# Retention and an ELU feed-forward layer: where the load and the attention of unit 3 stand among the weight loads and FFN1

## The chip, the cores and the metric

The kernel runs on one core of one Trainium2 chip. The metric is the device time of one execution in microseconds (us), the median of several runs. The profile is of one execution, and its times count from the start of its span.

## The reference

Two layers follow each other. The first is a retention: causal attention without a softmax, in which the score of a query and a key is weakened by a head's decay to the power of their distance. The second is a feed-forward layer with an ELU between two matrix products.

```python
# q, k, v: (8 batches, 8 heads, 576 positions, 64), float32
scores = 1/sqrt(64) * matmul(q, k.transpose(0, 1, 3, 2))
gamma = 1.0 - 2.0 ** (-5.0 - arange(8))              # one decay per head
rel = pos[:, None] - pos[None, :]
Dmat = where(rel >= 0, gamma[:, None, None] ** rel, 0.0)
ret = matmul(scores * Dmat, v)
x = ret.transpose(0, 2, 1, 3).reshape(4608, 512)     # tokens by heads * 64
h = x @ w_in                                         # w_in (512, 2048)
g = where(h > 0, h, exp(minimum(h, 0)) - 1)          # ELU
out = g @ w_out                                      # w_out (2048, 512), out float32
```

## The kernel before

The 4608 tokens are 36 units of 128 tokens. The attention of a unit has these steps: `load` (q, k and v of all heads, three or six transfers issued on SyncE), `cast` (q and k to bf16), `scale_v` (v times a decay, on GpSimd), `turn` (transposes of q and k on TensorE and the copies back), `scores`, `masks` (the causal mask and the move out of PSUM, on VectorE), `inter` (the part from earlier units through a state), `state` (its update), `intra` (the product of masked scores and v), `put_x` (the result times a decay, into the input of the feed-forward layer) and `state_out` (the state, copied for the next unit). The feed-forward layer takes units in groups; `ffn1` computes tiles of h with the ELU, and `ffn2` the products with w_out. In FFN1 of group 0 (units 0 to 2) each of the 16 tiles is 128 of the 2048 features by 384 tokens, and four tiles use one part of w_in.

```python
GROUPS = [[0, 1, 2], [3], [4], [5], [6, 7], [8, 9], [10, 11, 12], [13, 14, 15]]
GROUPS += [list(range(u, u + 4)) for u in range(16, NU, 4)]
raw = ctx.enter_context(tc.tile_pool(name="raw", bufs=8))
ps_h = ctx.enter_context(tc.tile_pool(name="ps_h", bufs=3, space=PSUM))   # ps_m, ps_s, ps_o, ps_st: 1 each
# ... (cut)
def load(u, after=None):
    qk = raw.tile([P, 2, H, D], FP32, name="rqk", tag="rqk")
    vv = raw.tile([P, H, D], FP32, name="rv", tag="rv")
    if after is not None:
        after.memset(qk[0:1, 0, 0, 0:1], 0.0)          # the load waits for this engine's place in order
    for p0, b, s0, n in place(u):
        for dst, src in ((qk[p0 : p0 + n, 0], q), (qk[p0 : p0 + n, 1], k), (vv[p0 : p0 + n], v)):
            nc.sync.dma_start(dst, src[b, :, s0 : s0 + n, :].rearrange("h p d -> p h d"))
# ... (cut)
def load_w_in(n):                                      # 512 of 2048 columns, float32 to bf16 on the way
    s = slice(n * 512, (n + 1) * 512)
    nc.gpsimd.dma_start(w_in_sb[:, :, s], w_in_v[:, :, s])

def load_w_out(c, f0, f1):                             # 256 of 512 columns
    s = (slice(None), slice(f0, f1), slice(c * 256, c * 256 + 256))
    nc.gpsimd.dma_start(w_out_sb[s], w_out_v[s])

for u in range(4):
    load(u)
# ... (cut)
def stretch(u, ahead=True):                            # attention of a unit, later in the kernel
    ahead = ahead and u + 1 < NU
    if ahead:
        scores(u + 1)
    inter(u); state(u); intra(u)
    if ahead:
        masks(u + 1)
    put_x(u)
    state_out(u)
# ... (cut)
def ffn1(g, ft, bank=None):
    pool, tag = bank or (ps_h, "ph")
    ph = pool.tile([P, 512], FP32, name="ph", tag=tag)
    # ... 4 matmuls for each 128 features
    nc.scalar.activation(e[:, w], ph[:, w], AF.Exp)
    nc.gpsimd.tensor_scalar(m[:, w], e[:, w], -1.0, 1.0, ALU.add, ALU.mult)
    # g = min(max(ph, 0), m) on VectorE, issued up to three slots later
# ... (cut)
def dummy(n):                                          # matmuls without use, 512 columns each
    dum = ps_m.tile([P, 512], FP32, name="dum", tag="pm")
    for _ in range(n):
        nc.tensor.matmul(dum, warm[:, :P], warm, start=True, stop=True)

def product(u):
    inter(u); state(u); intra(u); put_x(u); state_out(u)
# ... (cut)
dummy(18)
cast(0, A, V); make_gx(); scale_v(0); turn(0, h); dummy(2)
for u in range(3):
    scores(u); inter(u); state(u); masks(u)
    if u < 2:
        cast(u + 1, A, G)
        if u == 0:
            load_w_in(0)
        scale_v(u + 1); dummy(3); turn(u + 1, h)
    else:
        for n in range(1, 4):
            load_w_in(n)
        load_w_out(0, 0, 8); load_w_out(0, 8, 16); load_w_out(1, 0, 16)
        dummy(3)
    intra(u); put_x(u); state_out(u); dummy(2)
cast(3, A, V)

for n in range(16):
    f1(0, n, m if n % 4 == 3 else None)                # one tile of FFN1 of group 0
    if n == 3: turn(3)
    if n == 5: scale_v(3)
    if n == 7: scores(3); masks(3, 0)
    if n == 8: masks(3, 1)
    if n == 9:
        load(4, nc.vector)
        for u in range(5, 12):
            load(u)
    if n == 11: product(3)
for n in range(4):
    f1(1, n, m if n == 3 else None)
finish()
for u, bank in enumerate((h, h, h, m)):
    ffn2_half(u, 0, bank)                              # FFN2 of units 0 to 3, columns 0 to 255
prep(4, A, G)                                          # cast and scale_v
ffn2_half(0, 1, h); turn(4); ffn2_half(1, 1, h); scores(4); masks(4); prep(5, A, G)
ffn2_half(2, 1, h); product(4); turn(5); ffn2_half(3, 1, m)
scores(5); masks(5); prep(6, A, G)
f1(2, 0); f1(2, 1); turn(6); f1(2, 2)
# then a list of slots: FFN1 of a group alternates with FFN2 of the group before it,
# and the attention of later units is put between them by a timetable (due, events)
```

(Statements that stand on lines of their own in the kernel are joined here with semicolons.)

Of the kernel before, what the change touches and what calls it, by code (L numbers as in the profile page):

```python
# [9 lines left out]
FP32 = mybir.dt.float32  # L10
# [7 lines left out]
def kernel(  # L18
# [9 lines left out]
    nc = tc.nc  # L28
# [4 lines left out]
    P = 128  # L33
# [66 lines left out]
        nc.gpsimd.dma_start(w_out_sb[s], w_out_v[s])  # L100


    for u in range(4):
        load(u)

    ident = const.tile([P, P], BF16, name="ident")
# [180 lines left out]
            xts[g][:, :, i * P : (i + 1) * P], os_[u], gx[:, :, s0 : s0 + P], ALU.mult  # L287
        )

    def stretch(u, ahead=True):  # L290

        ahead = ahead and u + 1 < NU
        if ahead:
            scores(u + 1)
        inter(u)
        state(u)
        intra(u)
        if ahead:
            masks(u + 1)
        put_x(u)  # L300
        state_out(u)


# [41 lines left out]
    def ffn2(g, s):  # L345
        it, part = divmod(s, 4)
        while late and (g, part * 4 + 3) >= late[0][4]:
            finish(slot[0] - late[0][0])
        if part == 0:
            pool, tag = ((ps_o, "o"), (ps_m, "pm"), (ps_h, "ph"))[it] if g == NG - 1 else (ps_m, "pm")  # L350
# [30 lines left out]

    V, A, G = nc.vector.tensor_copy, nc.scalar.copy, nc.gpsimd.tensor_copy

    def dummy(n):
        dum = ps_m.tile([P, 512], FP32, name="dum", tag="pm")
        for _ in range(n):
            nc.tensor.matmul(dum, warm[:, :P], warm, start=True, stop=True)  # L387

# [28 lines left out]
    for u in range(3):  # L417
        scores(u)
        inter(u)
        state(u)  # L420
        masks(u)
        if u < 2:
            cast(u + 1, A, G)
            if u == 0:
                load_w_in(0)
            scale_v(u + 1)
            dummy(3)
            turn(u + 1, h)
        else:
            for n in range(1, 4):  # L430
                load_w_in(n)
            load_w_out(0, 0, 8)
            load_w_out(0, 8, 16)
            load_w_out(1, 0, 16)
            dummy(3)
        intra(u)
        put_x(u)
        state_out(u)
        dummy(2)
    cast(3, A, V)  # L440


    def f1(g, n, bank=None):
        k = 512 // (P * len(GROUPS[g]))
        ffn1(g, k * n, bank)

    for n in range(16):
        f1(0, n, m if n % 4 == 3 else None)
        if n == 3:
            turn(3)  # L450
        if n == 5:
            scale_v(3)
        if n == 7:
            scores(3)
            masks(3, 0)
        if n == 8:
            masks(3, 1)
        if n == 9:
            load(4, nc.vector)
            for u in range(5, 12):  # L460
                load(u)
        if n == 11:
            product(3)
    for n in range(4):
        f1(1, n, m if n == 3 else None)
    finish()
# [8 lines left out]
    prep(5, A, G)  # L475
    ffn2_half(2, 1, h)
    product(4)
    turn(5)
    ffn2_half(3, 1, m)
    scores(5)  # L480
    masks(5)
    prep(6, A, G)
    f1(2, 0)
    f1(2, 1)
    turn(6)
    f1(2, 2)


    slots, start, now = [(f1, 2, 3, 1.0)], {}, 1.0
    for g in range(3, NG + 1):  # L490
        f1s, f2s = [], [(ffn2, g - 1, s, 1.0) for s in range(4 * len(GROUPS[g - 1]))]
        if g < NG:
            per = 4 // len(GROUPS[g])
            f1s = [(f1, g, s, per * len(GROUPS[g]) / 4) for s in range(NFT // per)]
        else:
            f2s = f2s[:-4]
        a, b = 0, 2 if g == 4 else 0
        slots += f2s[:b]
        now += b
        start[g] = now  # L500
        while a < len(f1s) or b < len(f2s):
            if b * len(f1s) <= a * len(f2s) and b < len(f2s) or a >= len(f1s):
                slots.append(f2s[b])
                b += 1
            else:
                slots.append(f1s[a])
                a += 1
            now += slots[-1][3]
    due = {5: 0.0}
    last = 5  # L510
    for g in range(4, NG):
        u1 = GROUPS[g][-1]
        for u in range(last + 1, u1 + 1):
            due[u] = due[last] + (start[g] - 1.0 - due[last]) * (u - last) / (u1 - last)
        last = u1
    events = []
    for u in range(5, NU):
        def at(share):
            return due[u] + share * (due[u + 1] - due[u])
        events.append((due[u], 0, u))  # L520
        if u + 2 < PE_TURNED:
            events += [(due[u], -1, u + 2), (at(0.5), 1, u + 2)]
        if PE_TURNED <= u + 3 < NU:
            events.append((at(0.4) if u + 2 < PE_TURNED else due[u], -1, u + 3))
    events.sort()

    now = 0.0
    for f, g, s, d in slots:
        while events and events[0][0] <= now + d / 2:
            _, kind, u = events.pop(0)  # L530
            if kind == -1:
                prep(u, *((A, G) if u < PE_TURNED else (V,)))
                if u >= PE_TURNED:
                    turn(u)
            elif kind == 1:
                turn(u)
            else:
                load_next()
                stretch(u)
# [34 lines left out]
```

## Time and profile before

| | before |
|---|---|
| median of 3 runs | 319.48 us (318.46 to 320.52) |
| span of the profiled execution | 318.0 us |
| granted TensorE clock, mean | 0.993 |
| first tile of FFN1 starts | 17.56 us |
| first product of FFN2 starts | 37.92 us |
| TensorE busy from 17.56 to 37.92 us | 17.85 of 20.36 us |

The page names the engines PE (TensorE), PEld (its weight loads), DVE (VectorE), ACT (ScalarE), POOL (GpSimd) and SP (SyncE); SPq and POOLq are the issue of transfers. An instruction is given by line of the kernel, operation and tiles: `ph` is FFN1's result in PSUM, `pm` and `pmh` are FFN2's, `dum` a dummy's, `tr` a transpose, `sc` the scores, `o` the attention's result, `st` the state, `xt` the input of the feed-forward layer, `m`, `e` and `g` steps of the ELU, `rqk` and `rv` what is loaded of q, k and v. A bracket at the end of a line gives the idle time before an instruction and who ended it. The page's slices are a fortieth of the span, 7.95 us each; PEclk is the granted clock of TensorE in tenths.

### The profile page before, as it was taken

To read this page: it belongs to the slowest core of one execution; us is meant where nothing else is said; L and a number is where in the kernel's file an instruction comes from. 1 tells how busy PE (TensorE), PEld (TensorE's weight loads), DVE (VectorE), ACT (ScalarE), POOL (GpSimd) and SP (SyncE) were. 2 spreads that over 40 slices of the span, in tenths; PEclk is the share of its full clock that TensorE was granted. 3 is DMA by queue.
4 is the path that set the end of the run, shared out by engine and by line. 5 is a ranking of instruction groups with operands and counts; after the bars stand their busy time and mean duration, and the time that the engine had idled before them with its cause. 6 is when DMAs were issued, how large, how long until landed. Compare 5 with 4: busy or idle time off the path is not lost.

```text
span 318.0 us, 7546 instructions
## 1 busy us (share of the span) xinstructions
PE 307.1 (97%) x2974; PEld 174.2 (55%) x3011; DVE 187.4 (59%) x297; ACT 136.9 (43%) x254; POOL 144.9 (46%) x223
## 2 busy tenths in 40 slices
PE   8969999999999999999999999999999999999995
PEld 3535888877766555555444444444444444444444
DVE  2755724667768777776677666666666655444300
ACT  6435514654643444444444444344444444344411
POOL 2875633555645655544554444444444433333300
PEclk9998999999999999999999999999999999999999
DMA  9999999999999998999999859778224200000111
GB/s 170 215 220 201 197 206 253 205 202 202 207 233 188 233 224 179 168 235 195 170 212 170 171 123 207 166 166 170 69 66 69 66 35 33 35 33 33 66 69 66
DMA packets 150195, 48.72 MB, mean 153 GB/s; under 512 B 138640, under 2 KB 146192, under 8 KB 150160
## 3 DMA queue, kind: packets, MB, share of 16 engines
q1 hardware_dynamic: 141888, 41.76, 67.5%
q0 software_dynamic: 6256, 4.19, 8.8%
q10 hardware_dynamic: 2016, 2.29, 2.2%
q8 instruction: 23, 0.38, 0.5%
q14 instruction: 12, 0.10, 0.1%
HBM read 36.70 MB, written 9.44 MB: 145 GB/s over the span
## 4 chain that ended last, share of the span: by engine, by line
PE 82%; DMA 6%; issue 3%; POOL 3%; SPq 2%; DVE 2%; ACT 0%; POOLq 0%; DVEq 0%
PE ph L329 35%; PE pm L354 31%; PE pmh L370 6%; PE sc L211 3%; DMA w_in_sb<-in_moe_w_in_dram 3%; PE o L273 2%; SPq L86 2%; PE st L256 2%; PE o L239 2%; DMA rv<-in_v_dram 2%; DMA qkT<-qkn 1%; POOL m L336 1%; POOL vn L177 1%; DVE pt L223 1%; PE tr L195 1%
## 5 line engine op out<-in xcount | busy, mean ns | idle before, releaser
L336 POOL TENSOR_SCALAR m<-e 128x512 bf16<-128x512 f32 (+1 forms) x156 | 93.7, 601 | 142.0 <-ACT e L334 137.1
L329 PE MATMUL ph<-xt,w_in_sb 128*128 128x512 bf16 (+3 forms) x816 | 146.5, 315 | 3.9 <-DMA w_in_sb<-in_moe_w_in_dram 2.3
L313 DVE SCALAR_TENSOR_TENSOR g<-ph,m 128x512 bf16<-128x512 f32 (+1 forms) x156 | 100.2, 647 | 81.3 <-POOL m L336 80.3
L334 ACT ACTIVATE e<-ph 128x512 f32<-128x512 f32 (+1 forms) x156 | 87.9, 564 | 124.6 <-PE ph L329 119.8
L354 PE MATMUL pm<-w_out_sb,g 128*128 128x512 bf16 x478 | 122.8, 379 | 1.5 <-issue 0.8
L329 PEld LDWEIGHTS <-w_in_sb 128*128 128x128 bf16 x832 | 71.8, 98 | 59.5 <-issue 4.0
L354 PEld LDWEIGHTS <-g 128*128 128x128 bf16 x496 | 47.8, 98 | 53.2 <-issue 0.2
L223 DVE TENSOR_TENSOR pt<-sc,mask 128x1024 bf16<-128x1024 f32 (+1 forms) x37 | 44.2, 1194 | 14.6 <-PE sc L211 14.4
L177 POOL TENSOR_TENSOR vn<-rv,gk 128x512 bf16<-128x512 f32 x36 | 37.9, 1052 | 1.8 <-DMA rv<-in_v_dram 1.3
L286 DVE TENSOR_TENSOR xt<-o,gx 128x512 bf16<-128x512 f32 x36 | 24.5, 682 | 3.1 <-PE o L273 2.9
L361 ACT COPY ot<-pm 128x512 f32<-128x512 f32 x31 | 18.1, 585 | 14.5 <-PE pm L354 13.8
L370 PE MATMUL pmh<-w_out_sb,g 128*128 128x256 bf16 (+1 forms) x176 | 18.3, 263 | 0.0
L265 ACT CAST sb<-st 128x256 bf16<-128x256 f32 x32 | 11.9, 373 | 13.1 <-PE st L256 11.3
L211 PEld LDWEIGHTS <-qkT 64*64 64x64 bf16 x576 | 9.2, 106 | 14.0 <-issue 7.8
L370 PEld LDWEIGHTS <-g 128*128 128x128 bf16 x176 | 15.7, 98 | 1.9
L168 DVE CAST qkn<-rqk 128x1024 bf16<-128x1024 f32 x24 | 16.6, 691 | 0.0
L211 PE MATMUL sc<-qkT 64*64 64x128 bf16 x576 | 15.1, 222 | 0.7 <-ACT qkT L197 0.5
L273 PE MATMUL o<-pt,vn 128*64 128x128 bf16 x288 | 14.4, 222 | 0.0
L375 DVE COPY oth<-pmh 128x256 f32<-128x256 f32 (+1 forms) x6 | 2.4, 400 | 18.0 <-PE pmh L370 18.0
L387 PE MATMUL dum<-warm 128*128 128x512 bf16 x32 | 11.2, 473 | 1.4 <-DVE warm L108 1.3
L239 PE MATMUL o<-qkT,sb 64*64 64x128 bf16 (+1 forms) x256 | 12.3, 214 | 0.0
L197 ACT COPY qkT<-tr 128x512 bf16<-128x512 bf16 x12 | 7.0, 585 | 9.6 <-DVE qkT L196 5.9
(40 smaller groups left out, 90.1 us busy)
## 6 DMA issues: line engine op xcount, KB each, us to landing
rqk<-in_q_dram SPq DMA_DIRECT2D x32, 256.0 KB, 4.7
rqk<-in_k_dram SPq DMA_DIRECT2D x32, 256.0 KB, 5.0
rv<-in_v_dram SPq DMA_DIRECT2D x32, 256.0 KB, 5.1
out_dram<-ot SPq DMA_DIRECT2D x27, 256.0 KB, 2.3
w_in_sb<-in_moe_w_in_dram POOLq DMA_DIRECT2D x4, 512.0 KB, 9.2
out_dram<-oth ACTq DMA_DIRECT2D x9, 128.0 KB, 4.0
w_out_sb<-in_moe_w_out_dram POOLq DMA_DIRECT2D x2, 512.0 KB, 14.6
w_out_sb<-in_moe_w_out_dram POOLq DMA_DIRECT2D x1, 1024.0 KB, 22.9
```

The costliest lines, as they stand in the source:

```text
L177: nc.gpsimd.tensor_tensor(n, rv, gk[:, u % R].unsqueeze(2).to_broadcast([P, H, D]), ALU.mult)
L211: nc.tensor.matmul(sc[j * 64 : (j + 1) * 64, i, hp], t[r, 1, hp, j * 64 : (j + 1) * 64], t[r, 0, hp], start=(hp == 0), stop=(hp == HP - 1) ...
L223: nc.vector.tensor_tensor(pts[u][:, s].rearrange("p i h t -> p (i h) t"), scs[u][:, s].rearrange("p i h t -> p (i h) t"), m.unsqueeze(1).t ...
L239: nc.tensor.matmul(o[rows, hp, :n], sbs[u][rows, hp], qkTs[u][rows, 0, hp, :n], start=(hp == 0), stop=False, skip_group_check=True,)
L273: nc.tensor.matmul(o[i * D : (i + 1) * D, hp], vns[u][:, h], pts[u][:, i, hp], start=(u % R == 0 and hp == 0), stop=(hp == HP - 1), skip_g ...
L286: nc.vector.tensor_tensor(xts[g][:, :, i * P : (i + 1) * P], os_[u], gx[:, :, s0 : s0 + P], ALU.mult)
L313: nc.vector.scalar_tensor_tensor(gt_, ph, 0.0, m, ALU.max, ALU.min)
L329: nc.tensor.matmul(ph[:, i * n : (i + 1) * n], w_in_sb[:, j, f : f + P], xts[g][:, j, :n], start=(j == 0), stop=(j == KJ - 1), skip_group_ ...
L334: nc.scalar.activation(e[:, w], ph[:, w], AF.Exp)
L336: nc.gpsimd.tensor_scalar(m[:, w], e[:, w], -1.0, 1.0, ALU.add, ALU.mult)
L354: nc.tensor.matmul(pm, gts[g, ft][:, it * P : (it + 1) * P], w_out_sb[:, ft], start=(ft == 0), stop=(ft == NFT - 1))
L370: nc.tensor.matmul(pm, gts[g, ft][:, it * P : (it + 1) * P], w_out_sb[:, ft, c0:c1], start=(ft == 0), stop=(ft == NFT - 1),)
```

## The change

It reorders the start of the kernel and the units 3 to 7. Unit 3 is no longer loaded first with units 0 to 2; w_in's second part is issued right after the first, then unit 3, then the third and fourth part from within FFN1, so that the parts of w_in come ahead of what is needed later. The attention of unit 3 is no longer spread over FFN1's tiles: it stands in one piece after tile 7, with eight dummies to keep TensorE at work while the copies and the mask product run. The loads of w_out are issued from within FFN1 rather than before it. Units 5 to 7 get other places for scores, mask product and product; in `stretch` the last unit of a group writes its `xt` before the next unit's mask product; group 2 accumulates FFN2 in a bank of `ps_h`. The arithmetic is the same.

```diff
-    for u in range(4):
+    for u in range(3):
         load(u)
 ...
-    def stretch(u, ahead=True):
+    def stretch(u):
+        if u + 1 < NU:
             scores(u + 1)
         inter(u)
         state(u)
         intra(u)
-        if ahead:
+        last = GROUPS[group_of[u][0]][-1] == u
+        if last:
+            put_x(u)
+        if u + 1 < NU:
             masks(u + 1)
-        put_x(u)
+        if not last:
+            put_x(u)
         state_out(u)
 ...
-            pool, tag = (... if g == NG - 1 else (ps_m, "pm")
+            pool, tag = (... if g == NG - 1 else (ps_h, "ph") if g == 2 else (ps_m, "pm")
 ...
-    def dummy(n):
-        dum = ps_m.tile([P, 512], FP32, name="dum", tag="pm")
+    def dummy(n, bank=(ps_m, "pm")):
+        dum = bank[0].tile([P, 512], FP32, name="dum", tag=bank[1])
 ...
     for u in range(3):
         scores(u)
         inter(u)
-        state(u)
+        if u == 2:
+            load(3, nc.vector)
         masks(u)
         if u < 2:
             cast(u + 1, A, G)
             if u == 0:
                 load_w_in(0)
+                load_w_in(1)
             scale_v(u + 1)
             dummy(3)
             turn(u + 1, h)
         else:
-            for n in range(1, 4):
-                load_w_in(n)
-            load_w_out(0, 0, 8)
-            load_w_out(0, 8, 16)
-            load_w_out(1, 0, 16)
             dummy(3)
+        state(u)
         intra(u)
         put_x(u)
         state_out(u)
         dummy(2)
-    cast(3, A, V)
 ...
-    for n in range(16):
+    o = (ps_o, "o")
+    for n in range(8):
         f1(0, n, m if n % 4 == 3 else None)
+        if n == 0:
+            load_w_in(2)
         if n == 3:
-            turn(3)
-        if n == 5:
-            scale_v(3)
-        if n == 7:
-            scores(3)
-            masks(3, 0)
-        if n == 8:
-            masks(3, 1)
-        if n == 9:
+            load_w_in(3)
+            cast(3, A, V)
+    turn(3)
+    scale_v(3)
+    dummy(3, o)
+    scores(3)
+    masks(3)
+    load_w_out(0, 0, 8)
+    load_w_out(0, 8, 16)
+    dummy(5, o)
+    product(3)
+    for n in range(8, 16):
+        f1(0, n, m if n % 4 == 3 else None)
+        if n == 10:
             load(4, nc.vector)
             for u in range(5, 12):
                 load(u)
         if n == 11:
-            product(3)
+            load_w_out(1, 0, 16)
 ...
     product(4)
+    ffn2_half(3, 1, m)
     turn(5)
-    ffn2_half(3, 1, m)
-    scores(5)
-    masks(5)
     prep(6, A, G)
     f1(2, 0)
     f1(2, 1)
+    scores(5)
+    masks(5)
+    f1(2, 2)
+    f1(2, 3, m)
+    product(5)
     turn(6)
-    f1(2, 2)
-    slots, start, now = [(f1, 2, 3, 1.0)], {}, 1.0
+    slots, start, now = [], {}, 0.0
 ...
-        a, b = 0, 2 if g == 4 else 0
+        a, b = 0, 3 if g == 4 else 0
 ...
-    due = {5: 0.0}
-    last = 5
+    due = {6: 6.0}
+    last = 6
 ...
-    events = []
-    for u in range(5, NU):
+    events = [(0.0, -1, 7), (2.0, 2, 6), (4.0, 1, 7)]      # prep 7, scores and masks 6, turn 7
+    for u in range(6, NU):
```

More of the change, by code (lines that the diff above doesn't have):

```diff
@@ L288, in put_x @@
         )
-    def stretch(u, ahead=True):
-        ahead = ahead and u + 1 < NU
-        if ahead:
+    def stretch(u):
+        if u + 1 < NU:
             scores(u + 1)
@@ L297, in stretch @@
         intra(u)
-        if ahead:
+        last = GROUPS[group_of[u][0]][-1] == u
+        if last:
+            put_x(u)
+        if u + 1 < NU:
             masks(u + 1)
-        put_x(u)
+        if not last:
+            put_x(u)
         state_out(u)
@@ L349, in ffn2 @@
         if part == 0:
-            pool, tag = ((ps_o, "o"), (ps_m, "pm"), (ps_h, "ph"))[it] if g == NG - 1 else (ps_m, "pm")
+            pool, tag = ((ps_o, "o"), (ps_m, "pm"), (ps_h, "ph"))[it] if g == NG - 1 else (ps_h, "ph") if g == 2 else (ps_m, "pm")
             acc[0] = pool.tile([P, DM], FP32, name="pm", tag=tag)
@@ L536 @@
                 turn(u)
+            elif kind == 2:
+                scores(u)
+                masks(u)
             else:
```

## The prediction

> **What bounds the kernel now.** I read the busy shares first, then who waited for whom on TensorE, then TensorE's instructions in order of time, then the same stretch in windows with the granted clock, and last the DMA queues.
>
> ```profile
> PE 307.1 (97%) x2974; PEld 174.2 (55%) x3011; DVE 187.4 (59%) x297; ACT 136.9 (43%) x254; POOL 144.9 (46%) x223
> PEclk9998999999999999999999999999999999999999
> ```
>
> TensorE bounds the kernel, and a change of order can win only what TensorE loses by idling, by running at a lower clock, or by doing dummies. The one digit below 9 lies in the fourth slice, at 24 to 32 us. The waits of TensorE over the whole span:
>
> ```profile
> PE ph L329 <- DMA w_in_sb<-in_moe_w_in_dram: 2.3, 1, 2.3
> PE ph L329 <- DVE xt L286: 0.5, 2, 0.3
> PE sc L211 <- ACT qkT L197: 0.5, 2, 0.2
> ```
>
> One wait is worth a change: 2.3 us for the second part of w_in. In order of time (start, duration, instruction, count):
>
> ```profile
> 20.15 0.61 PE L195 MATMUL tr<-ident,qkn 128*128 128x128 bf16 x8
> 23.02 4.46 PE L329 MATMUL ph<-xt,w_in_sb 128*128 128x384 bf16 x16 [2.26 <-DMA w_in_sb<-in_moe_w_in_dram]
> ...
> 27.76 2.14 PE L329 MATMUL ph<-xt,w_in_sb 128*128 128x384 bf16 x12
> ```
>
> The last row is the healthy rate: 12 matmuls of 384 columns in about 1.94 us (161 ns each, also what 215 ns for 512 columns scales to). The 16 after the wait should take 2.58 us and took 4.46, so 1.9 us more are lost. The windows (length, busy times, then the granted clock, DMA share, GB/s) say why:
>
> ```profile
> 20.00:22.00 2.00, 0.76 (x10) 0.52 (x8) 1.61 (x5) 0.77 (x3) 1.91 (x4) 1.00 1.24 206
> 22.00:24.00 2.00, 0.98 (x4) 0.51 (x5) 0.81 (x2) 0.50 (x1) 0.00 (x0) 0.82 1.24 206
> 24.00:26.00 2.00, 2.00 (x7) 0.91 (x6) 0.49 (x1) 0.82 (x2) 0.51 (x1) 0.50 1.25 205
> 26.00:28.00 2.00, 2.00 (x25) 1.06 (x24) 0.74 (x3) 1.07 (x3) 1.76 (x3) 0.83 1.43 201
> ```
>
> The idle stretch was followed by some 3.4 us at half clock (missing shares 0.18 + 0.50 + 0.17, times 2 us = 1.7 us lost). So the late w_in costs 2.3 + 1.9, about 4.2 us. All else on TensorE from 40 us on is small: 0.3 us for xt, 0.2 for qkT, 0.8 of issue gaps.
>
> Why w_in is late is seen in the DMA queues, one microsecond at a time (packets, MB, share); q1 carries q, k and v, q0 the weights. At 13 to 14, 17 to 18 and 19 to 20 us:
>
> ```profile
> q0 software_dynamic: 192, 0.20, 117.4%
> q1 hardware_dynamic: 24, 0.01, 4.7%
> ...
> q1 hardware_dynamic: 919, 0.23, 133.4%
> q0 software_dynamic: 2, 0.00, 1.2%
> ...
> q0 software_dynamic: 197, 0.20, 120.6%
> q1 hardware_dynamic: 20, 0.01, 3.4%
> ```
>
> The queues take turns in order of issue. Units 0 to 2 fill the engines to about 12.3 us, w_in part 0 to 15, unit 3 to 18.1 (0.79 MB), and only then part 1, issued at 14.62, moves and lands 8.36 us later, at 22.98.
>
> **What the Trainium skill says.** (1) "TensorE: Matmul & The Clock Gate", section "What's actually happening": the array runs at half clock after about one idle window of 3.4 us and needs a busy one to return. The trace agrees: 0.82, 0.50, 0.83 add up to one such window. (2) "DMA: Bandwidth & Descriptors", "Issuing engines are not separate DMA queues": all issuers share the same 16 engines, so issuing from another one makes no bandwidth. The trace agrees: q0 with q1 stays near 0.2 MB per us. (3) Same page, "Queues, rings and completion order": each engine alternates between its rows packet by packet. The trace differs: q1 gets 0.00 to 0.01 MB per us while q0 has a backlog. The trace decides, and I work with turns in order of issue. (4) Same page, "Latency and other measured facts": engines 7 and 15 are usually slower. It fits that landings lag behind the bulk (part 1's bytes are through at about 20.7 by 0.205 MB per us, it lands at 22.98), though no view here names the engine.
>
> **The change part by part.** (a) *Part 1 of w_in ahead of unit 3.* GpSimd issues it right after part 0, at about 10.7 instead of 14.62. This puts 0.8 us more on GpSimd ahead of vn of unit 1; vn of unit 2 waits for data until 13.57 anyway, and state(1) now stands later, so the first FFN1 tile stays at about 17.5. The data: part 0 from 12.3 to 14.9, part 1 (0.524 MB at 0.205) to 17.4, landing before 20, while tile 4 wants it at 17.56 + 4 x 0.645 = 20.1. The wait of 2.3 us goes, and with it the idle window and the 1.9 us of half clock: **-4.2 us**.
>
> (b) *Unit 3 in one piece after tile 7, with dummies.* The eight added dummies are 8 x 0.215 = **+1.7 us** of TensorE time. They cover turn to scores (three, 0.65 us, against the copies of qkT, 0.42 on VectorE and 0.58 on ScalarE) and scores to intra (five, 1.07, plus inter and state 0.5, against one mask product of 1.22). The copies and vn of unit 3 stand behind the elu of tiles 6 and 7 (ScalarE 0.49, GpSimd 0.51 each, and two weight issues of 0.8 to 1.0 between), so I add **+0.5 us** of gaps. Unit 3's data run from 17.4 to 21.0, landing by about 22.5; its casts come after tile 3, near 21, just in time. Parts 2 and 3 issue near 20 and 22 and land near 25 and 28, for tiles 8 and 12 at about 26.5 and 29. The two small waits of before in this stage (0.25 + 0.25) are taken as gone: **-0.4**.
>
> Sum to the start of FFN2 (37.92 before): -4.2 + 1.7 + 0.5 - 0.4 = -2.4, so about 35.5.
>
> (c) *w_out later.* First half: issued near 26 to 27.5, data from 28.5 to 33.6, wanted from 35.5: hidden. Second half (1.05 MB): issued after tile 11, near 31, behind some 0.5 MB of unit 4 issued from 29.5. It landed at 41.5 before; with 0.5 MB ahead of it (2.5 us) that becomes about 43 to 44.5, and is wanted 4 x 1.75 = 7.0 us after FFN2's start, at 42.5. Then turn(4) needs unit 4, which before was there at about 44 and is not much earlier. So part of (a) may be handed back here: **+0.6 us** as a mean of nothing and 2.
>
> (d) *Units 4 to 7.* Scores of unit 5 now stand two FFN1 tiles behind turn(5), so the 0.24 us at 58.05 goes; xt of a group's last unit is written before the next mask product (1.22 us), so the 0.26 us at 72.39 and like delays go; the accumulator of group 2 takes a bank of another pool, leaving two for FFN1 during four slots, which suffices: one tile plus two FFN2 slots are 2.6 us, the elu chain 0.6 + 0.62 + 0.69. **-0.5 us**.
>
> Sum: -2.4 + 0.6 - 0.5 = -2.3 us, so 319.48 - 2.3 = **317.2 us**.
>
> **The rivals.** *R1: a wait for w_out or unit 4 takes the place of the one for w_in.* For it: the first 50 us move 0.2 MB per us without pause, and the same bytes must be there before FFN2 gets to unit 4; GpSimd's cast of unit 4 waited until 43.71 before:
>
> ```profile
> 43.71 0.61 POOL L171 CAST qkn<-rqk 128x512 bf16<-128x512 f32 x1 [4.24 <-DMA rqk<-in_k_dram]
> ```
>
> Against it: TensorE used that only at 46.66. If it holds in full, 2 us of the gain are lost, and a wait over 2 us could bring half clock again: 319 to 321. *R2: unit 3 in one piece is itself a hole.* If its data land at 23 or later, or vn waits behind the weight issues on GpSimd, ScalarE, VectorE and GpSimd stop behind the casts and the tiles stall for banks: 1 to 2 us, giving 318.5. *R3: all is hidden.* No dummy costs what I count, since they fill time in which TensorE would have waited for the mask product anyway, and the later stages gain at each of twelve group ends: -4 us, 315.5. *R4: nothing changes,* since the chain is bound by DMA to 45 us: 319.3.
>
> **Range and chances.** The main sum has a gain of 2.3; R1 takes up to 3 from it, R3 adds 1.7. The three times before spread over 2 us (318.46 to 320.52), and a median is good to about 0.6. I take 315.2 to 319.2. Faster by over 2% means under 313.1, a gain of 6.4, more than all that TensorE loses in this stage: 0.03. Slower by over 2% means over 325.9; a second hole with half clock costs 4 to 5, so it would take two: 0.02.
>
> **What would show it.** Right: no wait of ph for w_in over 0.5 us, the fourth slice of the clock back at 9, tile 4 following tile 3 at once, the last tile of group 0 ending near 32 instead of 34.3, the first pmh at 35 to 36 instead of 37.92, the 32 recorded dummies become about 40. R1 shows as a wait of pmh for w_out or of tr for qkn between 40 and 47 us; R2 as waits of tr, sc or o in 22 to 28 us, and a clock digit below 9 there. I am wrong if FFN2 starts early and the end does not move: then a later stage gives the gain back, to be found by comparing the start of each group.

## The result, and the profile after

The changed kernel takes 324.0 us in the median (323.6 to 324.7), beside 319.0 for the kernel before on the same chip: a ratio of 1.0152, with a 95% interval of 1.0110 to 1.0194. The prediction was 317.2 us with a range up to 319.2; it was wrong in sign.

The page of the profile after, TensorE's row and clock:

```profile
PE 307.8 (96%) x2981; PEld 174.1 (54%) x3019; DVE 187.2 (58%) x297; ACT 137.1 (43%) x254; POOL 144.7 (45%) x223
PEclk9999999999999999999999999999999999999999
```

The clock is whole and TensorE is busy for 0.7 us more than before, in a span 3.9 us longer (321.9 after 318.0). So most of the loss is idle time. Who ended it, in the list of waits on TensorE (total us, times, longest):

```profile
PE ph L332 <- DVE g L316: 2.9, 4, 1.0
PE tr L195 <- ACT qkn L171: 1.9, 1, 1.9
```

The wait for w_in is gone, as meant. In its place FFN1's tiles wait four times for `g`, that is for a bank of PSUM that the ELU of an earlier tile must empty; the transposes of unit 4 wait 1.9 us for a cast on ScalarE. TensorE in order of time shows where:

```profile
17.76 3.43 PE L332 MATMUL ph<-xt,w_in_sb 128*128 128x384 bf16 x20 [0.24 <-DVE xt L286]
21.68 0.81 PE L332 MATMUL ph<-xt,w_in_sb 128*128 128x384 bf16 x4 [0.48 <-DVE g L316]
23.10 1.46 PE L332 MATMUL ph<-xt,w_in_sb 128*128 128x384 bf16 x8 [0.61 <-DVE g L316]
...
26.14 0.42 PE L211 MATMUL sc<-qkT 64*64 64x128 bf16 x16 [0.49 <-ACT qkT L197]
...
28.61 5.41 PE L332 MATMUL ph<-xt,w_in_sb 128*128 128x384 bf16 x32
34.89 3.73 PE L332 MATMUL ph<-xt,w_in_sb 128*128 128x128 bf16 x64 [0.86 <-DVE g L316]
38.46 9.15 PE L373 MATMUL pmh<-w_out_sb,g 128*128 128x256 bf16 x80
49.53 0.62 PE L195 MATMUL tr<-ident,qkn 128*128 128x128 bf16 x8 [1.92 <-ACT qkn L171]
```

Read down the starts: FFN2 begins at 38.46, not at the 35.5 of the prediction and not even at the 37.92 of before, and the transposes of unit 4 stand at 49.53 where they stood at 46.66. The rest follows from the starts of each unit's scores: after minus before is -1.3 us for unit 3, +2.9 for unit 4, +3.7 for unit 10, +3.9 for unit 17 and for all that follow. So 2.9 of the 3.9 us arise before 50 us and 1.0 between unit 4's scores and 130 us.

### The profile page after: what moved, and what is told of

Same layout as the page of the kernel before. It is cut to its first block, busy times and chain, and to the rows that moved or that the text cites. A ratio compares the mean times of both kernels' runs of the same rounds, so it can differ in the third digit from the quotient of the medians.

```text
span 321.9 us, 7559 instructions
## 1 busy us (share of the span) xinstructions
PE 307.8 (96%) x2981; PEld 174.1 (54%) x3019; DVE 187.2 (58%) x297; ACT 137.1 (43%) x254; POOL 144.7 (45%) x223
## 4 chain that ended last, share of the span: by engine, by line
PE 79%; DMA 7%; DVE 4%; SPq 4%; issue 2%; POOL 1%; ACT 1%; ACTq 0%; DVEq 0%; POOLq 0%
PE ph L332 34%; PE pm L357 32%; DMA rqk<-in_k_dram 7%; SPq L86 4%; PE sc L211 3%; PE pmh L373 3%; PE o L273 2%; PE st L256 2%; PE o L239 2%; DVE pt L223 2%; PE tr L195 1%; DVE g L316 1%; DVE xt L286 1%; POOL w_out_sb L100 1%; POOL m L339 0%
## 5 line engine op out<-in xcount | busy, mean ns | idle before, releaser
L332 PE MATMUL ph<-xt,w_in_sb 128*128 128x512 bf16 (+3 forms) x816 | 144.8, 313 | 4.2 <-DVE g L316 2.9
L223 DVE TENSOR_TENSOR pt<-sc,mask 128x1024 bf16<-128x1024 f32 x36 | 44.0, 1222 | 13.6 <-PE sc L211 13.5
L390 PE MATMUL dum<-warm 128*128 128x512 bf16 x40 | 12.7, 451 | 1.3 <-DVE warm L108 1.3
```

The lines of the kernel that those rows point to most:

```text
L223: nc.vector.tensor_tensor(pts[u][:, s].rearrange("p i h t -> p (i h) t"), scs[u][:, s].rearrange("p i h t -> p (i h) t"), m.unsqueeze(1).t ...
L332: nc.tensor.matmul(ph[:, i * n : (i + 1) * n], w_in_sb[:, j, f : f + P], xts[g][:, j, :n], start=(j == 0), stop=(j == KJ - 1), skip_group_ ...
```

## The experiments

Times are medians; a ratio is to the kernel before on the same chip, with its 95% interval. For e8 and e11 both leave out executions in a slower state (two of seven, one of five). The first theory after the result: (1) unit 4's cast of q stands on ScalarE behind two stores of FFN2's results and comes late; (2) the new places of units 4 to 7 cost a wait at 82 us; (3) FFN1's waits come from weight issues on GpSimd between the steps of the ELU. The rival to all: the bytes that must be there by 46 us set the pace, and a wait taken away comes back as another. Where the quoted expectations use letters, the lines after them say in words what held.

### The changed kernel again (e6)

No edit.

> The changed kernel itself once more, unaltered, so that the runs beside it have it from the same chip: 323 to 324.5 us by all theories.

Measured: 323.44 us, 1.0145 (1.0100 to 1.0189). The loss is stable, but its waits are not: this profile has two of them ahead of unit 4's transposes.

```profile
46.65 1.92 PE L373 MATMUL pmh<-w_out_sb,g 128*128 128x256 bf16 x16 [1.52 <-DMA w_out_sb<-in_moe_w_out_dram]
49.62 0.62 PE L195 MATMUL tr<-ident,qkn 128*128 128x128 bf16 x8 [1.05 <-ACT qkn L171]
```

Here FFN2 starts earlier, at 37.98 instead of 38.46, w_out's second half is there later, at 46.6 instead of 45.6, and TensorE waits 1.52 us for it and 1.05 us for the cast. The transposes start at the same time, 49.6 after 49.5. So the unaltered change already has the wait that the rival names.

### Unit 4's q cast on VectorE (e1)

```diff
-    prep(4, A, G)
+    prep(4, V, G)      # in the changed kernel
```

> The changed kernel with one word altered: the cast of unit 4's q runs on VectorE instead of ScalarE. Theory Q (ScalarE's queue): TensorE's wait of 1.92 us before the transposes of unit 4 is there because the cast stands behind the issue of an output store on ScalarE (issued at 48.48 us), which waits for a load of unit 5 to land, not because unit 4 is missing; GpSimd cast k of unit 4 at 44.57 and could go on. Then the wait goes and the time falls by 1.0 to 2 us, to 322 to 323. Theory D (data): unit 4 lands too late for all engines. Then the transposes still start near 49.5 us and the time stays at 324.

Measured: 322.17 us, 1.0105 (1.0081 to 1.0128), 1.3 us below e6. In the profile after, GpSimd casts unit 4's k early and ScalarE its q late; these are the rows of GpSimd, and then of ScalarE (ACTq is its issue of a transfer), in order of time:

```profile
44.57 0.61 POOL L171 CAST qkn<-rqk 128x512 bf16<-128x512 f32 x1 [4.55 <-DMA rqk<-in_k_dram]
```

```profile
48.48 0.34 ACTq L379 DMA_DIRECT2D out_dram<-oth  x1
48.86 0.62 ACT L171 CAST qkn<-rqk 128x512 bf16<-128x512 f32 x1 [1.73 <-DMA rqk<-in_k_dram]
```

Unit 4's k was there before 44.6; the store issued at 48.48 is what the cast of q stood behind. Unit 4's q itself had landed at 41.6, and in e1 VectorE could read it at 43.62. In the program as built, transfers issued by SyncE and ScalarE take eight completion semaphores in turn (a completion semaphore is the counter that tells of a transfer's landing), and an issue waits for the transfer that had its semaphore before. In the trace this store has the semaphore of unit 5's k, issued at 37.95 and landed at 48.40; ScalarE waits for that semaphore, and the store follows at 48.48. The transfer of k that the bracket names is this one. With the cast on VectorE (VectorE's row in e1):

```profile
43.62 0.42 DVE L171 CAST qkn<-rqk 128x512 bf16<-128x512 f32 x1
```

The wait of 1.9 us is gone and the transposes start at 46.69, as early as before. Theory (1) holds for the cast; w_out's second half was there in time in this execution, at 44.9.

### Part (a) alone in the kernel before (e2), and with unit 3's attention later (e12)

```diff
-    for u in range(4):            # e2 alone
+    for u in range(3):
         load(u)
 ...
+        if u == 1: load(3, nc.vector)     # e2 alone
 ...
                 load_w_in(0)
+                load_w_in(1)              # e2 and e12; in e12 unit 3's turn, scores
 ...                                       # and product stand two to four tiles later
-            for n in range(1, 4):
+            for n in range(2, 4):
```

> The kernel before with part (a) of the change alone: part 1 of w_in is issued right after part 0, unit 3 is loaded after it (released by VectorE in unit 1), the other weight loads, the spread attention of unit 3 and all the rest stay as they were. Theory G (the gain of (a) is real and was eaten by the other parts): the wait of 2.3 us for w_in and the half clock go, the first product of FFN2 starts near 34 us instead of 37.92, and up to 4 us are won: 315 to 317. Rival H (hidden): FFN2 then waits for w_out's second half or for unit 4, so the transposes of unit 4 start no earlier than 46 us, and the time stays at 319.

> The kernel before with part 1 of w_in issued right behind part 0, unit 3 loaded where it was, and the spread attention of unit 3 two to four tiles later (casts after tile 5, transposes after 7, scores after 10, product after 13); no dummies, no other change. Theory G: the wait of 2.3 us for w_in goes without a new one, FFN2 starts near 35 us; what is won at the end is 1 to 2 us, 317.5 to 318.5, as turn(4) can't come before unit 4's bytes. Rival: unit 3 shares the transfer engines with the weights and comes later still (it did in the second run), its casts stop ScalarE and VectorE, and nothing is won: 319.5 or more.

Measured: e2 326.88 us, 1.0215 (1.0152 to 1.0279); e12 323.01 us, 1.0110 (1.0092 to 1.0128). e2 met neither of its expectations; e12 met its rival's, at a higher cost. Part (a) alone costs: unit 3 now shares the DMA engines with the other weights, issued all at once near 15 us, and is waited for. The waits on TensorE in e2:

```profile
PE tr L195 <- DVE qkn L171: 4.7, 1, 4.7
PE tr L195 <- ACT qkn L171: 3.5, 1, 3.5
```

Unit 3's loads were issued from 13.33 us, ahead of w_in's third part, and its v landed only at 33.3. The DMA queues of e2 from 25 to 28 us (packets, MB, share):

```profile
q0 software_dynamic: 673, 0.38, 87.5%
q1 hardware_dynamic: 679, 0.17, 43.4%
```

In this stretch both queues move the same number of packets, and the weights more than twice the bytes. e12 gives unit 3 more time and still waits 5.0 us for it. So an early issue does not secure early arrival: what else is queued matters as much.

### The late part alone (e3), undone (e4), and its `stretch` alone (e14)

```diff
-    turn(5); ffn2_half(3, 1, m)          # e3: the kernel before with the
-    scores(5); masks(5)                  # change's hunks from stretch and
+    ffn2_half(3, 1, m); turn(5)          # after product(4) on, cut here
 ...                                      # e4: the changed kernel without them
-        put_x(u)                         # e14: the kernel before with
+        if not last: put_x(u)            # the hunk in stretch alone
```

> The kernel before with only the late part of the change: the order of units 4 to 7, the xt of a group's last unit before the next mask product, the bank of group 2. As predicted it should win 0.5 us (318.5). As the trace of the changed kernel suggests (one new wait of 0.98 us at 82.04 us on VectorE's g, against waits of 0.24 and 0.26 that are gone) it should lose 0.5 to 1 us: 319.5 to 320.

> The changed kernel with its late part undone (units 4 to 7 in the order of before), the complement of the third run. If the late part costs 0.5 to 1 us, this falls to 323 to 323.5; if it wins 0.5 us, it rises to 324.5. The wait before the transposes of unit 4 (1.92 us) stays in either case.

> The kernel before with one piece of the late part: xt of a group's last unit is written ahead of the next unit's mask product. The wait of 0.26 us for xt at 72.39 us goes; if nothing else moves, 319.2 instead of 319.5, which is hardly to be told from no change. If it is this piece that made the late part slower, the time rises by 1 us.

Measured: e3 320.04 us, 1.0011 (0.9987 to 1.0035); e4 322.38 us, 1.0079 (1.0055 to 1.0103); e14 319.65 us, 1.0019 (0.9994 to 1.0044). The profile of e3, TensorE in order of time:

```profile
22.92 2.77 PE L332 MATMUL ph<-xt,w_in_sb 128*128 128x384 bf16 x16 [1.96 <-DVE g L316]
...
78.22 1.92 PE L332 MATMUL ph<-xt,w_in_sb 128*128 128x256 bf16 x16 [0.98 <-DVE g L316]
```

The last row is the wait of 0.98 us that the changed kernel has at 82.04: VectorE does a mask product of 1.23 us and an `xt` of 0.68 before the two `g` that FFN1 waits for. In the profiles it costs about 1.0 us, in e4 against e6 1.1. In e3 the interval holds nothing as well as 1.1; but all 12 executions of e3 had a mean clock of 0.998 or more, and against the 28 of 40 of the kernel before that had it too (median 318.9) e3 is 1.1 us slower. The hunk in `stretch` alone (e14) has no such wait in its profile. So the late part is a loss of about 1 us, and not the gain of 0.5.

The first row says something else. Up to unit 4 e3 is the kernel before, and tile 4 starts at 22.92 as it did at 23.02 there (the bracket names `g`, but w_in's second part, too, landed only at 22.87), but the 16 matmuls take 2.77 us and not 4.46: no half clock followed, and FFN2 starts at 36.54. Of 106 executions of the kernel before in these experiments, 77 had a mean clock of 0.998 or more (median 318.8 us) and 29 of 0.996 or less (median 320.7): the profiled one that I predicted from, with 0.993, was of the minority. (One stretch as in that profile loses 1.7 us, 0.5% of the span: an estimate that fits a mean clock of 0.995.) The wait for tile 4 varies too: 2.26 us there, 1.96 in e3, 1.55 in e14, 1.16 in e18.

### No dummies (e5)

```diff
     turn(3); scale_v(3)
-    dummy(3, o)
     scores(3); masks(3); load_w_out(0, 0, 8); load_w_out(0, 8, 16)
-    dummy(5, o)
     product(3)
```

> The changed kernel without the eight dummies around the scores of unit 3. If the dummies cost what the prediction counted (8 x 0.215 us of TensorE time on the path), the time falls by 1.7 us. If they only fill time in which TensorE would have waited for the copies and the mask product (rival R3 of the prediction), it stays within 0.5 us and the same stretch shows waits of tr, sc and o instead. If the idle time brings half clock, it rises by 1 us or more.

Measured: 323.69 us, 1.0136 (1.0095 to 1.0178), about the time of e6; three of the four executions had a clock of 1.0 and a median of 323.44, e6's own. The waits in the profile, which is of the fourth:

```profile
PE sc L211 <- ACT qkT L197: 2.0, 3, 1.1
...
PE o L273 <- DVE pt L223: 0.8, 1, 0.8
```

They grew from 0.9 and from nothing to 2.0 and 0.8: the 1.7 us of dummies stood where TensorE would have waited. Their cost was nothing; the piece itself has the gaps. In this one execution half clock followed, though no single wait was longer than 1.13 us: the 32 matmuls behind the piece take 7.09 us instead of 5.41.

```profile
27.82 7.09 PE L332 MATMUL ph<-xt,w_in_sb 128*128 128x384 bf16 x32
```

### Weight issues out of the ELU (e7)

```diff
+        if u == 2:                       # before FFN1
+            for n in (2, 3): load_w_in(n)    # each after a VectorE memset of its tile
 ...
-        if n == 0: load_w_in(2)
-        if n == 3: load_w_in(3)          # cast(3, A, V) stays here
 ...
     load_w_out(0, 8, 16)
+    load_w_out(1, 0, 16)
     dummy(5, o)
 ...
-        if n == 11: load_w_out(1, 0, 16)
```

> The changed kernel with GpSimd's weight issues taken out of the ELU chain of FFN1: parts 2 and 3 of w_in are issued after xt of unit 2 is written (held by a one-element write of VectorE) and before the first m, and the second half of w_out right behind the first, while GpSimd waits for the mask product of unit 3. Theory G: the issues (0.8 to 1.8 us each) hold back m, so g, so the PSUM banks; the waits of TensorE on g in FFN1 of group 0 (0.48 + 0.61 + 0.86 = 1.95 us) go, FFN2 starts about 2 us earlier, near 36.5, and the time falls by up to 2 us, less what a wait for unit 4 gives back. Rival: the banks are short because of the casts and the mask product on VectorE and ScalarE; then the waits on g stay and the time stays at 324.

GpSimd in the changed kernel, in order of time, shows what the issues stand among:

```profile
19.66 0.82 POOL L96 DMA_DIRECT2D w_in_sb<-in_moe_w_in_dram  x1
...
21.91 0.98 POOL L96 DMA_DIRECT2D w_in_sb<-in_moe_w_in_dram  x1
...
26.69 1.84 POOL L100 DMA_DIRECT2D w_out_sb<-in_moe_w_out_dram  x2
...
32.52 1.17 POOL L100 DMA_DIRECT2D w_out_sb<-in_moe_w_out_dram  x1
```

VectorE in the same stretch, where `g` is written:

```profile
21.06 0.56 DVE L316 SCALAR_TENSOR_TENSOR g<-ph,m 128x384 bf16<-128x384 f32 x1 [0.78 <-POOL m L339]
22.15 0.43 DVE L171 CAST qkn<-rqk 128x512 bf16<-128x512 f32 x1 [0.53 <-DMA rqk<-in_k_dram]
22.50 2.02 DVE L316 SCALAR_TENSOR_TENSOR g<-ph,m 128x384 bf16<-128x384 f32 x4
...
34.28 1.97 DVE L316 SCALAR_TENSOR_TENSOR g<-ph,m 128x384 bf16<-128x384 f32 x4 [1.11 <-POOL m L339]
```

The first and the third of FFN1's three waits (0.48 and 0.86 us) end on a `g` that waited for `m` behind an issue of 0.82 or 1.17 us on GpSimd. The second (0.61) ends on a `g` that stood behind the cast of unit 3's k, for which VectorE itself waited: the rival's engine, and a late transfer. In e1, e4, e6, e9 and e10 this second wait is 0.29 us, and the three together 1.65.

Measured: 323.94 us, 1.0147 (1.0112 to 1.0181). FFN1's waits for `g` before FFN2 fell from 1.95 to 0.45 us, so theory (3) is right for most of them, but the time is unchanged. New waits in e7's profile:

```profile
PE st L256 <- POOL vn L177: 1.6, 1, 1.6
...
PE pmh L373 <- DMA w_out_sb<-in_moe_w_out_dram: 0.8, 1, 0.8
```

Unit 3's v now comes late behind the weights, and then w_out does. This is the rival: a wait removed comes back as another.

### Mends together (e10, e11, e8)

```diff
# e10: late part as before, and
-    prep(4, A, G)
+    prep(4, V, G)
# e11: e10 without the two dummy lines.  e8: e10 with the edit of e7.
```

> The changed kernel with its late part undone and the cast of unit 4's q on VectorE. If the two are separate, their worths (about 1.2 and 1.9 us) add up: 323.5 - 3.1 = 320.4, within 1 us of the kernel before. What is left then is FFN1 of group 0: the dummies (1.7 us) and the waits on g (1.95 us) against the wait for w_in that is gone (2.3 us).

> The run beside it (late part undone, cast on VectorE) without the eight dummies. With the wait on ScalarE's queue gone, time won ahead of FFN2 can reach the end. If the dummies cost 1.7 us of TensorE time, up to 1.7 us are won against the run beside it; if they only fill waits, or if w_out's second half and unit 4 set the pace here (1.14 us of waiting for w_out in the fifth run), less than 0.5 us.

> The changed kernel with three mends at once: late part undone, cast of unit 4's q on VectorE, weight issues out of the ELU chain. If the three causes are separate, their worths add up: 1.6 (fourth run) + 1.9 (first run) + 1.5 to 2 (third run of this set) bring 324 down to 318.5 to 319, level with the kernel before. If one of them only hides another, it stays above 320.5.

Measured: e10 320.66 us, 1.0059 (1.0007 to 1.0111); e11 322.59 us, 1.0087 (1.0057 to 1.0117); e8 322.52 us, 1.0105 (1.0052 to 1.0158). The two mends of e10 add up, as expected: it is 2.8 us below e6, beside 1.3 (e1) and 1.1 (e4) for each alone. What is left above the kernel before belongs to the start up to FFN2, which e10 reaches at 37.99 us, and e3 and e14, with the start of the kernel before and a whole clock, at 36.54 and 36.39. Neither dropping the dummies nor moving the issues brings it back. e11 is even 1.9 us above e10; its profile has a wait of 1.42 us for w_in at the first tile that e10's has not, so this is not the dummies' worth. e8 stays above 320.5: one cause hides another.

### Unit 5 held back (e9)

```diff
         if n == 10:
             load(4, nc.vector)
-            for u in range(5, 12): load(u)
 ...
     # after FFN2's first half-column product of unit 0
+    load(5, nc.vector)
+    for i in range(6, 12): load(i)
```

> The changed kernel with the loads of unit 5 and later held until VectorE has copied the first half product of FFN2 (near 41 us) instead of following unit 4's loads at once. In the built program the transfers of SyncE and ScalarE share eight completion semaphores in turn, and each issue waits for the transfer eight places earlier; in the changed kernel the stores of units 2 and 3 stand behind loads of units 4 and 5, in this one behind units 3 and 4 only. Theory Q (the stores on ScalarE wait for loads of unit 5, and the cast of unit 4 stands behind them): the stores are issued as soon as their copies are done, TensorE's wait of 1.9 us before the transposes of unit 4 goes, and 2 us are won: 321.5 to 322.5. Theory D (the bytes of w_out and unit 4 alone are too late): the wait stays, 323.5 or more.

Measured: 322.39 us, 1.0084 (1.0059 to 1.0109). The time is 1.0 us below e6, as theory Q expected, but the profile does not show Q's reason. The wait of `tr` for the cast is gone, and the list of waits has one of 1.8 us of `pmh` for w_out in its place, ending at 46.88. ScalarE still casts q only at 48.13, behind a store that waited for unit 4's v; the wait for w_out hides it. Holding these loads did not bring w_out earlier than it was wanted.

### Unit 3 spread again (e13), the ELU partly on VectorE (e15, e16)

```diff
# e13: e10, with unit 3's attention spread as in the kernel before, without its dummies
+        if n == 8:  turn(3); scale_v(3)
+        if n == 9:  scores(3); masks(3, 0); load_w_out(0, 0, 8); load_w_out(0, 8, 16)
+        if n == 10: masks(3, 1)          # and the loads of unit 4, as in the changed kernel
+        if n == 12: product(3)
# e15: e10, e16: e13, with some steps of the ELU moved
+    eng = nc.vector if g == 0 and ft in (1, 4, 12) else nc.gpsimd     # e16: 1, 4, 10, 11, 12
+    eng.tensor_scalar(m[:, w], e[:, w], -1.0, 1.0, ALU.add, ALU.mult)
```

> The tenth run's kernel (late part undone, cast on VectorE) with the attention of unit 3 spread over tiles 8 to 12 as in the kernel before, and no dummies there; loads in the order of the change. Theory P (the one piece is the cost): 4.2 us between tiles 7 and 8 become the 1.5 us of unit 3's own matmuls, FFN2 starts up to 2.7 us earlier, and the time falls by 1 to 2.5 us, to 318 to 319.7. Theory G (GpSimd sets the pace, as 16 m, one vn and five issues are some 14 us): the waits on g grow by what the pause no longer hides and the time stays within 0.7 us of the tenth run.

> The tenth run's kernel with the ELU step m of tiles 1, 4 and 12, the three that stand right behind weight issues on GpSimd, on VectorE; every transfer stays where it is. Theory G: the waits on g in FFN1 of group 0 (0.51 + 0.29 + 0.86 us) go and FFN2 starts 1.0 to 1.7 us earlier; at the end 0.5 to 1.5 us are won, or nothing if w_out and unit 4 set the pace there. Rival: VectorE is as late as GpSimd; the waits on g stay.

> Both together: attention of unit 3 spread, m of tiles 1, 4, 10, 11 and 12 on VectorE, late part undone, cast on VectorE. If one piece and issues are all that the changed start costs, FFN2 starts near 34 to 35 us and the time falls to 317 to 318.5, below the kernel before. If the bytes set the pace, TensorE waits for w_out or unit 4 between 40 and 47 us (2 us or more) and the time stays at 319.5 to 320.5.

Measured: e13 324.65 us, 1.0161 (1.0122 to 1.0201); e15 323.11 us, 1.0122 (1.0045 to 1.0199); e16 325.00 us, 1.0170 (1.0109 to 1.0231). In e15 two waits for `g` in FFN1 stay (0.91 and 0.85 us, beside e10's 0.51, 0.29 and 0.86): VectorE is as late as GpSimd. e13 met neither expectation. It gains less than theory P said, FFN2 starts at 37.39, 0.6 us earlier than in e10, and then loses more than that:

```profile
48.70 3.47 PE L370 MATMUL pmh<-w_out_sb,g 128*128 128x256 bf16 x16 [3.39 <-DMA w_out_sb<-in_moe_w_out_dram]
```

TensorE waits 3.39 us for w_out's second half and then runs 16 matmuls at half clock (3.47 us for 1.92). e16 waits 4.0 us at the same place, and all executions of both had a mean clock of 0.994 or 0.995. An earlier FFN2 is worth nothing while w_out is not there.

### w_out ahead of unit 4 (e17), and late w_out alone (e18)

```diff
# e17: e13, with
         if n == 9:
+            load_w_out(1, 0, 16)         # right after the first half
-        if n == 10:
+        if n == 13:                      # loads of units 4 to 11
             load(4, nc.vector)
# e18: the kernel before, with
-            load_w_out(1, 0, 16)         # issued with the first half
+        if n == 11: load_w_out(1, 0, 16)
```

> The spread kernel again, with both halves of w_out issued together in tile 9 and the loads of units 4 and later held until tile 13. If the order of the bytes is what held the start of FFN2 (w_out and the loads of unit 4 sharing the DMA engines after 30 us): the waits for w_out, 0.61 and 3.39 us there, fall below 0.5 us together, unit 4 is still there by 46 us, and the time is 319.5 to 321.5 us. If it is not the order but the number of bytes up to FFN2, a wait of 1.5 us or more stays, for w_out or for unit 4 in its place, and the time is 322.5 us or more.

> The kernel before, with only the second half of w_out issued after tile 11 of FFN1 instead of with the first. If the later issue of w_out costs by itself: a wait for w_out of 1 to 2 us ahead of the second half of the sums of FFN2's first product, at about 45 us, and 320.5 to 321.5 us. If it costs only together with the loads of unit 4 earlier in the changed kernel: no wait for w_out over 0.3 us, and 318.8 to 319.8 us.

Measured: e17 321.76 us, 1.0125 (1.0059 to 1.0191); e18 319.85 us, 1.0034 (1.0016 to 1.0051). TensorE in e17:

```profile
46.22 1.92 PE L370 MATMUL pmh<-w_out_sb,g 128*128 128x256 bf16 x16 [1.63 <-DMA w_out_sb<-in_moe_w_out_dram]
```

A wait of 1.63 us is left with w_out ahead of unit 4, as the second expectation said, and the time lies between the two: the order of the bytes explains part of e13's wait. For the rest, the window of e17 from 28 to 30 us (last two columns: DMA share, GB/s) points to a late start more than to the number of bytes, since w_out is issued only from 27.98 us:

```profile
28.00:30.00 2.00, 1.14 (x8) 0.47 (x6) 1.47 (x3) 0.98 (x2) 2.00 (x4) 1.00 0.24 28
```

For two microseconds the DMA engines move 28 GB/s. At the 185 or so of its later windows that is, as an estimate, some 0.3 MB, or 1.7 us, not moved: about the wait. The changed kernel in this window and the one ahead of it:

```profile
26.00:28.00 2.00, 1.80 (x29) 0.96 (x29) 1.23 (x1) 0.09 (x1) 2.00 (x3) 1.00 0.84 143
28.00:30.00 2.00, 2.00 (x33) 1.29 (x28) 1.28 (x3) 0.84 (x2) 0.54 (x1) 1.00 0.79 102
```

Before, they moved 201 and 195 GB/s here. Summed over the windows from 20 to 44 us, the kernel before moved 4.73 MB and the changed one 4.27: 0.46 MB less, some 2.3 us of transfer at 0.2 MB per us. The profiles of e3 and e14 have 4.89 and 4.85 MB, those of e4, e6 and e10 4.21 to 4.29.

e18 fell between its two expectations. It has no wait for w_out, but it has the changed kernel's other wait. GpSimd, and then ScalarE:

```profile
40.84 0.61 POOL L171 CAST qkn<-rqk 128x512 bf16<-128x512 f32 x1 [1.96 <-DMA rqk<-in_k_dram]
```

```profile
46.08 0.34 ACTq L376 DMA_DIRECT2D out_dram<-oth  x1
46.46 0.62 ACT L171 CAST qkn<-rqk 128x512 bf16<-128x512 f32 x1 [1.58 <-DMA rqk<-in_k_dram]
```

Unit 4's k is cast at 40.84, its q 5.6 us later, behind a store; TensorE waits 0.91 us for it. So a later issue of w_out is enough to bring that wait. Alone it costs 1.1 us (0.5 to 1.6); where the mean clock was 0.998 or more (12 of 20 executions, 19 of 23 of the kernel before) it is 0.6.

## Why the prediction was wrong, by its own steps

| step | predicted | measured in the two profiles |
|---|---|---|
| (a) wait for w_in | -2.3 | -2.3 |
| (a) half clock | -1.9 | -1.9 in the profiled pair, nothing in the median |
| (b) eight dummies | +1.7 | 1.8 recorded (seven of them), no cost (e5) |
| (b) gaps less two small waits | +0.1 | +2.2 |
| start of FFN2 | 35.5 us | 38.46 us |
| (c) w_out later (start of FFN2 to the transposes of unit 4) | +0.6 | +2.3 |
| (d) units 4 to 7 | -0.5 | about +1.0 |

**(a)** The wait went as predicted. The half clock was real in the profile I had, but it is a matter of the single execution: e3 idled 1.96 us at the same place and kept its clock, the profiled run before idled 2.26 and lost it. The Trainium skill ("TensorE: Matmul & The Clock Gate", section "What's actually happening") gives about one idle window of 3.4 us. The runs here show half clock after single waits of 2.26 and 3.39 us, none after 1.96 (e3), and in e5 after several short ones, the longest 1.13 us; e11 has the same short waits in this piece and keeps its clock. So no limit for a single wait comes out of them. A median in which 77 of 106 runs don't have it can't gain it. The predicted gain for the median should have been the wait alone, 1.2 to 2.3 us by the four profiles with this start, and not 4.2.

**(b) is the step that failed first.** FFN1 idles 0.48 + 0.61 + 0.49 + 0.86 = 2.44 us, where before two waits of 0.25 were left besides w_in's. I had put +0.5 for all gaps. e7 and the rows of VectorE show the cause of the 1.95 us for `g`: 1.34 us come from weight issues on GpSimd between the steps of an ELU that frees FFN1's banks, and 0.61 from VectorE, which stands at the cast of unit 3's k until that lands. I had reckoned with two issues and data "just in time", and called the second rival, a hole in this place, 1 to 2 us. It was 2.2 in this profile, and 0.3 less in the five others with the same start. Of what is left of the start, 0.2 us is a later start of tile 0; some 0.5 us I did not take apart.

**(c) had the right place and half of the mechanism.** I looked for a late w_out and allowed 2 us at most. In the profile after, w_out's second half landed at 45.6 us, just in time; in e6, the same kernel, TensorE waited 1.52 us for it. What I had not thought of was the cast of q, late by 1.92 and 1.05 us in these two, because ScalarE stood in an issue that waits for an unrelated load (e1). That load shared the DMA engines with w_out, in a way that I had argued away. I had read from the kernel before that the queues take turns in order of issue, against the Trainium skill ("DMA: Bandwidth & Descriptors", section "Queues, rings and completion order"), which has each engine alternate between its queues packet by packet. Here the counts fit the page. The queues of the changed kernel from 39 to 43 us:

```profile
q0 software_dynamic: 940, 0.48, 86.9%
q1 hardware_dynamic: 937, 0.23, 45.6%
```

Equal packets, twice the bytes for the weights: w_out's second half, although issued at 32.5 us, after unit 4's first loads, took two thirds of the bandwidth from the loads of units 4 and 5. Such equal counts are not the rule everywhere: the q, k and v queue stood almost still at 13 to 14 us in the kernel before, which is what misled me, and in e2 from 28 to 33 us it moved 14 to 80 packets in each microsecond beside 351 to 384, while unit 3's v was still under way. Why was not settled.

**(d)** had the wrong sign: it brings a wait of 0.98 us. Behind it stand a mask product and an `xt` ahead of two `g` on VectorE, but the kernel before has the same order at 77 to 80 us without a wait, and `stretch` alone (e14) has none. So it comes with the new places of the units or the bank for group 2; which of them was not separated. One reading was wrong too: the scores at 58.05 us, whose wait of 0.24 was to go, are unit 6's, not unit 5's.

**The rival R1 came true, and deeper than it was put.** It said that the bytes up to unit 4 set the pace and that another wait takes the place of the one for w_in. It shows in the unaltered change (1.5 us for w_out in e6), and each mend of the start showed it: w_out 0.8 us (e7), 1.8 (e9), 4.0 (e13, e16), 1.6 (e17). What it missed is that the change also makes the bytes later. With the weight issues spread over FFN1 the engines move 143 and 102 GB/s from 26 to 30 us, in a stage in which the kernel before moved about 200. This is read from the windows; no run here has the changed order with full queues. The prediction read that the first 50 us move 0.2 MB per us without pause, and didn't ask whether the new places of the issues keep it so.

Against e3's profile, which has the kernel before's start with its clock whole, the changed kernel is at the transposes of unit 4 3.8 us later (49.53 after 45.72; e14 has them at 45.26, which gives 4.3); with 1.0 for the late part this is 4.8 to 5.3, beside 5.0 between the medians.

What stays open: how the last 0.6% of e10 (0.1 to 1.1%), some 1.8 us, divides between FFN1's gaps and the bytes. No version here beats the kernel before; e3 and e14 equal it within their intervals.

## What to carry to other kernels

A wait for a transfer in a stage where the DMA engines never rest can be a sign of too many bytes, and reordering then only moves it, as in each mend here: before counting the gain, add up the bytes that the next two waits need, and look whether every new place of an issue keeps the queues full. An issue is also work of the engine that makes it and stands in that engine's order, so put it neither among steps that free another engine's buffers nor ahead of a cast that the critical path needs. A cost that one profiled execution shows, such as half clock, enters the median only if most executions have it.

## What the runs showed of the hardware that was not expected

- In two stretches the two DMA queues moved equal numbers of packets, whichever was issued first (940 and 937 from 39 to 43 us of the changed kernel, 673 and 679 from 25 to 28 us of e2); since a packet of w_out carries 0.51 KB and one of q, k and v 0.25, w_out got two thirds of the bytes. In others they did not (14 to 80 beside 351 to 384 in e2).
- A store on ScalarE was issued 0.08 us after an unrelated load of SyncE with the same completion semaphore had landed (48.48 after 48.40; 48.56 after 48.48 in e6; 46.08 after 46.01 in e18).
- One issue of a weight load takes 0.82 to 1.17 us of GpSimd (the five in and around FFN1 of the changed kernel).
- Without any change to the kernel, 29 of 106 executions had a mean clock of 0.996 or less and took 1.9 us longer in the median.
